# Reciprocal denominators carried by DMAs through a DRAM scratch instead of spread by matmuls, with the output matmuls gathered in one burst

## The chip, the core and the metric

The kernel runs on one core of a Trainium2 chip. The metric is the device time of one execution in microseconds (us), and medians are quoted. The **span** is what one profiled execution shows from its first to its last instruction; the time is a little longer than the span.

## The reference

A linear attention (16 heads of 28 columns) is multiplied by a gated feed-forward branch and added to the input. There are 2048 tokens, 448 columns and 1792 hidden columns, in bfloat16.

```python
xn = layernorm(x)
q, k, v = heads(xn @ wqkv)
pq, pk = phi(q), phi(k)            # phi(t) = (t + 1 if t > 0 else exp(t)) + 1e-6
kv  = sum over tokens of pk outer v
z   = sum over tokens of pk
den = pq . z + 1e-6                # one number for each token and head
s = (pq @ kv / den) @ wo
h = relu(xn @ w1 + b1) ** 2
g = silu(h @ w2 + b2)
out = x + s * g
```

## The kernel before

Everything is kept transposed: `pqT[:, c, tokens]` holds 128 columns of pq on the partitions, for c = 0 to 2, and `pqx` holds the last 64. `kv` and `wo` are folded into one matrix `msb`, so that the attention output of a tile of 128 tokens (an "S tile") is pq / den times `msb`. A "gate tile" is 14 accumulating matmuls with `w2`. The division happens on pq, before the S matmuls, so the reciprocal of each (head, token) must reach the 28 partitions of its head. The kernel before does this on TensorE, with a 0/1 matrix `ehd` (row = head, column = column of the model):

```python
def spread(c):                     # ... cut: c == 3 uses two half-width matmuls for each g
    for g in range(NG):            # 32 rows of the array each: another array tiling
        r = slice(32 * g, 32 * g + 32)
        last = e.matmul(ps(bufs[g])[:, 0:512], ehd[r, c * P : (c + 1) * P], rden[r, :], ...)
    ...
    for g in range(NG):            # and VectorE multiplies pqT by what stands in PSUM
        e.tensor_tensor(out=sl, in0=sl, in1=ps(bufs[g])[:, 0:n], op=ALU.mult)
```

`ehd` is built at the start by one memset and four selects on GpSimd. Each S tile ends in a gate product (VectorE, from PSUM), an addition of x and an output DMA on the SyncE queue, which issues in order:

```python
def gate(si, b, lo, hi, k, final):
    add("dve", ... ob = ps(b)[:, lo:hi] * gs ...)
    add("dve" if final else "pool", ... ob = ob + x_tok[:, si, lo:hi] ...)   # pool is GpSimd
    dma("sp", tok(out, si, si + 1)[:, 0, lo:hi], ob, ...)
```

The second half of TensorE's program, in order:

```python
den(); quads("H3.8 H3.9 H3.10 H3.11")
# gate tiles 0..3 follow
spread(0); fold_wv(); ggs(4); spread(1); [fold_wo(c) for c in range(4)]; ggs(5)
spread(2); ggs(6); ggs(7); spread(3)
ss4_rests_last(0); ss4(1)                 # S groups of four tiles
for si in range(8, 15): ggs(si)           # gate tiles
ss4(2)
us = s_tails([(12, 0, D), (13, 0, D), (14, 0, D), (15, 0, D)])
for k in range(3):
    s_main(us[k], k, k > 0)               # third argument False: tile 12 is added on GpSimd
gg_part(15, 0, 224); s_main(us[3], 3, True, 0, 224)
gg_part(15, 224, D); s_main(us[3], 4, True, 224, D)
```

The list is laid out for the engines by a scheduler inside the kernel's program, so "in order" means the order on TensorE. One detail matters later: in both kernels every DMA has a semaphore of its own.

Of the kernel before, what the change touches and what calls it, by code (L numbers as in the profile page):

```python
# [6 lines left out]
ALU = mybir.AluOpType  # L7
AF = mybir.ActivationFunctionType

P = 128  # L10
S, D, F = 2048, 448, 1792
NT, NG, NF = S // 128, S // 512, F // 128
NH, DH = 16, 28
HC = 4
PD = 112
NGB, NOB = 8, 8

LAT = 0.12
PSUM_BANKS = 8
# [280 lines left out]
def bass_recurrent_scan__linear_attn_block__dense_activation_squared_relu__prompt_kernel(  # L300
    nc, A_x, A_wqkv, A_wo, B_x, B_w1, B_b1, B_w2, B_b2, out
):
    with ExitStack() as es:
# [8 lines left out]
        zmask = sb("zmask", [P, 5, 32], f32)  # L312
        ones = sb("ones", [P, 1], bf)
        wz = sb("wz", [P, P], bf)
        ehd = sb("ehd", [P, D], bf)
        x_tok = sb("x_tok", [P, NT, D], bf)
        wqh = sb("wqh", [P, 64], bf)
        xn = sb("xn", [P, NT, 512], bf)
# [19 lines left out]
        eps5 = sb("eps5", [P, 1], f32)  # L338
        r2 = sb("r2", [P, NF, S], bf)
        kvm = sb("kvm", [P, 4, D], bf)  # L340
        msb = sb("msb", [P, 4, D], bf)
        zsb = sb("zsb", [P, 5, 32], bf)
        lnd = sb("lnd", [P, 512], f32)[:, :]
        rden = sb("rden", [P, 512], bf)
# [9 lines left out]
        def free_ap(ap, dims):  # L354
            return bass.AP(tensor=ap.tensor, offset=ap.offset, ap=[ap.ap[0]] + dims)
# [4 lines left out]
        def select(view, name, pattern, base, cm, fill, op=ALU.is_ge, dur=0.3, after=()):  # L360
            pool(
                lambda e, _: e.affine_select(
                    out=view, in_=view, pattern=pattern, compare_op=op, fill=fill, base=base, channel_multiplier=cm
                ),
                [name], [name, *after], dur=dur,
            )
# [5 lines left out]
        def vset(ap, val, name, again=False, dur=0.08):  # L372
            add("dve", lambda e, _: e.memset(ap, val), [name] if again else [], [name], dur)
# [2 lines left out]
        pr.ops[-1].prio = -1e6  # L376
        vset(hmask[:, :], 1.0, "hmask", dur=0.15)
        vset(zmask[:, :, :], 1.0, "zmask", dur=0.2)
        vset(ehd[:, :], 0.0, "ehd", dur=0.3)
        vset(kvm[:, :, :], 0.0, "kvm", dur=1.0)  # L380
        pool(lambda e, _: e.memset(ones[:, :], 1.0), ["ones"], dur=0.1)
        pool(lambda e, _: e.memset(eps6[:, :], 1e-6), ["eps6"], dur=0.1)
# [12 lines left out]
        def head_masks(after):  # L395
            hv = hmask[:, :].rearrange("p (b j) -> p b j", b=HC)
            select(hv, "hmask", [[-DH, HC], [0, DH]], 0, 1, 0.0, after=after)
            select(hv, "hmask", [[DH, HC], [0, DH]], DH - 1, -1, 0.0, after=after)
            ev = ehd[:, :].rearrange("p (h j) -> p h j", h=NH)
            for g in range(NG):  # L400
                select(ev, "ehd", [[-1, NH], [0, DH]], -32 * g, 1, 1.0, ALU.not_equal, dur=0.6, after=after)

        tok = lambda t, lo, hi: t[0].rearrange("(p s) d -> p s d", s=NT)[:, lo:hi, :]

        def dma(eng, dst, src, writes, nbytes, reads=(), dur=0.45):
            op = add(eng, lambda e, _: e.dma_start(dst, src), reads, writes, dur, nbytes=nbytes)
            if eng == "act":
                op.prio = -1000.0 + len(pr.ops)
# [442 lines left out]
        def fold_wo(c):  # L851
            b = Buf("M")
            hs = {0: (0, 1), 1: (1, 2), 2: (2, 3), 3: (3,)}[c]

            def f(e, _):
                last = None
                for o in range(1 if c < 3 else 2):
                    dst = ps(b)[:, 0:D] if c < 3 else ps(b)[64 * o : 64 * o + 64, 0:D]
                    wd = P if c < 3 else 64
                    for h in hs:  # L860
                        last = e.matmul(  # L861
                            dst, kvm[0:PD, h, c * P : c * P + wd], w_o[0:PD, h, :], start=(h == hs[0]),
                            stop=(h == hs[-1]),
                        )
                return last

            add("pe", f, ["kvd", "kvm", "wo"], [b], 0.19 * len(hs) * (2 if c == 3 else 1))

            def ev(e, eng):
                if eng == "dve":  # L870
                    return e.tensor_copy(msb[:, c, :], ps(b)[:, 0:D])
                return e.activation(out=msb[:, c, :], in_=ps(b)[:, 0:D], func=AF.Copy)

            add("dve", ev, [b], [("msb", c)], 0.62, alts=[("act", 0.55)])

        denb = Buf("DEN")

        def den():
            def f(e, _):
# [26 lines left out]
                [denb, "eps6", "actw"], ["lnd"], 0.7,  # L906
            )
            add(
                "act", lambda e, _: e.activation(out=rden[:, :], in_=lnd, func=AF.Exp, scale=-1.0), ["lnd"],
                ["rden"], 0.65,  # L910
            )

        def spread(c):
            bufs = [Buf("RB") for _ in range(NG)]

            def f(e, _):
                last = None
                for g in range(NG):
                    r = slice(32 * g, 32 * g + 32)
                    if c < 3:  # L920
                        last = e.matmul(  # L921
                            ps(bufs[g])[:, 0:512], ehd[r, c * P : (c + 1) * P], rden[r, :], start=True, stop=True
                        )
                    else:
                        for o in (0, 1):
                            d4 = rden[r, o * P : o * P + P]
                            last = e.matmul(
                                ps(bufs[g])[64 * o : 64 * o + 64, 0:256], ehd[r, 384:448],
                                free_ap(d4, [[2 * P, 2], [1, P]]), start=True, stop=True,
                            )  # L930
                return last

            add("pe", f, ["rden", "ehd"], bufs, 0.22).mode = "row32"
            for g in range(NG):
                if c < 3:
                    sl, n, nm = pqT[:, c, g * 512 : (g + 1) * 512], 512, ("pq", g, c)
                    rd, wr = [nm], [nm]
                else:
                    sl = pqx[:, g // 2, 2 * (g % 2) : 2 * (g % 2) + 2, :].rearrange("p a b -> p (a b)")
                    n = 256  # L940
                    rd, wr = [("pqx", g // 2)], [("pqy", g)]
                add(
                    "dve",
                    lambda e, _, sl=sl, b=bufs[g], n=n: e.tensor_tensor(  # L944
                        out=sl, in0=sl, in1=ps(b)[:, 0:n], op=ALU.mult
                    ),
                    [bufs[g]] + rd, wr, 0.68 if c < 3 else 0.41,
                )

        def gg(si):  # L950
# [80 lines left out]
        def ss4(i, final=()):  # L1031
            t = 4 * i
            pe_four(*(sunit(si, si in final) for si in (t, t + 2, t + 1, t + 3)))
# [182 lines left out]
        for i in range(12, 16):  # L1216
            zsum(i)
        quads("Q2.0 H3.4 Q2.1 H3.6 Q2.2 H3.5 Q3.0 H3.7 Q3.1 H3.12 Q3.2 H3.13")
        qx(0)
        qx(1)  # L1220
        token_sum(3)
# [2 lines left out]
        z_cols()  # L1224
        token_sum(2)
        den()
        quads("H3.8 H3.9 H3.10 H3.11")
        silu_set()
        for si in range(4):
            silu(si)  # L1230
# [1 line left out]
        def ggs(si):  # L1232
            gg(si)
            silu(si)

        spread(0)
        fold_wv()
        ggs(4)
        spread(1)
        for c in range(4):  # L1240
            fold_wo(c)
        ggs(5)
        spread(2)
        ggs(6)
        ggs(7)
        spread(3)
        ss4_rests_last(0)
        ss4(1)
        for si in range(8, 15):
            ggs(si)  # L1250
        ss4(2)
        us = s_tails([(12, 0, D), (13, 0, D), (14, 0, D), (15, 0, D)])
        for k in range(3):
            s_main(us[k], k, k > 0)
        gg_part(15, 0, 224)
        s_main(us[3], 3, True, 0, 224)
        gg_part(15, 224, D)
# [31 lines left out]
```

## Time and profile before

| | before |
|---|---|
| time, median of 6 runs | 146.93 us (146.86 to 147.61) |
| span of the profiled execution | 145.1 us |
| last denominators' start to last S matmul's start | 50.76 us, TensorE never waiting |
| last S matmul's start to last output issue | 1.99 us |
| last output issue to the span's end | 2.1 us |

Where TensorE makes nearly the whole chain that ended last, a change elsewhere is worth only what TensorE no longer does and what happens behind its last matmul. So the reader is to measure slots, from one start to the next: durations overlap, as the ends of matmuls are modelled. The prediction below shows the lines.

### The profile page before, as it was taken

How to read it: one execution, taken by the hardware profiler on the slowest of the kernel's cores; microseconds unless marked ns; L12 is line 12 of the kernel's file. 1: busy time of each engine (PE TensorE's matmuls, PEld its weight loads, DVE VectorE, ACT ScalarE, POOL GpSimd, SP SyncE). 2: the span in 40 equal slices, each digit the busy share in tenths (PEclk: the TensorE clock that was granted, in tenths of full speed). 3: DMA queues.
4: the chain of work that ended last, by engine and by line, in shares of the span. 5: the costliest groups of instructions: out<-in, count | busy, mean ns of one | idle time of the engine just before them, and what ended most of it. 6: DMA issues, size and time to landing. Idle time of an engine off the chain costs nothing.

```text
span 145.1 us, 2851 instructions
## 1 busy us (share of the span) xinstructions
PE 140.2 (97%) x1134; PEld 72.5 (50%) x1134; DVE 95.7 (66%) x218; ACT 78.2 (54%) x150; POOL 36.5 (25%) x55
## 2 busy tenths in 40 slices
PE   7999999999999999999999999999999999999990
PEld 7774444444455444444444454464444455554490
DVE  5869989899985177678999500089847913123792
ACT  3618897988884198869879412598411012212010
POOL 2123025470000487003540000000000991000590
PEclk9999999999999999999999999999999999999999
DMA  3977899920744100000000000000000232000034
GB/s 94 315 240 234 209 183 374 340 84 0 52 97 103 41 5 0 0 0 5 2 0 0 5 0 0 0 5 2 0 0 0 65 104 88 0 0 0 5 127 127
DMA packets 16025, 10.53 MB, mean 73 GB/s; under 512 B 7500, under 2 KB 15628, under 8 KB 16012
## 3 DMA queue, kind: packets, MB, share of 16 engines
q1 hardware_dynamic: 15824, 10.28, 26.6%
q8 instruction: 9, 0.15, 0.4%
q10 hardware_dynamic: 188, 0.07, 0.2%
q14 instruction: 4, 0.03, 0.1%
HBM read 6.94 MB, written 1.84 MB: 60 GB/s over the span
## 4 chain that ended last, share of the span: by engine, by line
PE 96%; DVE 1%; ACT 1%; issue 0%
PE pb L957 28%; PE pb L716 26%; PE pb L624 7%; PE pb L785 6%; PE pb L650 6%; PE pb L1026 6%; PE pb L712 3%; PE pb L1114 3%; PE pb L979 2%; PE pb L1099 1%; PE pb L664 1%; PE pb L861 1%; PE pb L791 1%; PE pb L921 1%; PE pb L813 1%; PE pb L883 1%
## 5 line engine op out<-in xcount | busy, mean ns | idle before, releaser
L957 PE MATMUL pb<-w,r 128*128 128x448 bf16 x210 | 40.6, 353 | 0.0
L716 PE MATMUL pb<-xT,w 64*128 64x512 bf16 (+1 forms) x291 | 38.3, 376 | 0.0
L683 ACT ACTIVATE r<-pb,b1f 128x512 bf16<-128x512 f32 x54 | 33.7, 691 | 6.7 <-PE pb L716 6.7
L957 PEld LDWEIGHTS pb<-w,r 128*128 128x128 bf16 x210 | 20.2, 98 | 19.5 <-issue 1.2
L1015 POOL TENSOR_TENSOR obuf<-obuf,x_tok 128x448 bf16<-128x448 bf16 x13 | 13.1, 1043 | 53.9 <-DVE obuf L1009 53.9
L999 ACT ACTIVATE gbuf<-gbuf 128x448 bf16<-128x448 bf16 x15 | 8.3, 579 | 26.2 <-DVE gbuf L966 26.1
L716 PEld LDWEIGHTS pb<-xT,w 64*128 64x128 bf16 (+1 forms) x291 | 14.2, 94 | 16.5 <-ACT r L683 0.4
L966 DVE TENSOR_TENSOR gbuf<-pb,b2b 128x448 bf16<-128x448 f32 x15 | 9.4, 625 | 19.3 <-PE pb L957 19.2
L634 POOL TENSOR_TENSOR zacc<-zacc,pk 128x448 f32<-128x448 f32 x13 | 14.5, 1116 | 18.9 <-DVE pk L614 18.4
L697 DVE TENSOR_TENSOR r<-r 128x512 bf16<-128x512 bf16 x37 | 17.4, 502 | 2.0 <-ACT r L683 1.9
L624 PE MATMUL pb<-w_qkv,xT 64*128 64x448 bf16 x112 | 13.2, 349 | 0.0
L944 DVE TENSOR_TENSOR pqT<-pqT,pb 128x512 bf16<-128x512 bf16 x12 | 7.4, 681 | 7.2 <-PE pb L921 7.2
L602 ACT ACTIVATE pk<-pb 128x448 bf16<-128x448 f32 x16 | 7.8, 541 | 7.7 <-PE pb L624 7.7
L698 ACT ACTIVATE r<-r 128x512 bf16<-128x512 bf16 x19 | 11.2, 633 | 0.0
L650 PE MATMUL pb<-xT,w_qkv 64*128 64x512 bf16 x84 | 11.0, 376 | 0.0
L1009 DVE TENSOR_TENSOR obuf<-pb,gbuf 128x448 bf16<-128x448 f32 (+1 forms) x17 | 9.0, 590 | 2.6 <-PE pb L1026 2.4
L716 PE MATMUL pb<-xT,w_1r 64*128 64x512 bf16 x56 | 10.3, 377 | 0.0
L614 DVE SCALAR_TENSOR_TENSOR pk<-pb,pk 128x448 bf16<-128x448 f32 x16 | 9.9, 624 | 0.5
L466 DVE BATCH_NORM_STATS2 st<-x_tok 128x6 f32<-128x448 bf16 x16 | 9.2, 614 | 1.4 <-DMA x_tok<-in_A_x_dram 1.4
L785 PE MATMUL pb<-pk,xn 128*128 128x448 bf16 x48 | 9.4, 353 | 0.0
L607 DVE TENSOR_SCALAR pk<-pk 128x448 bf16<-128x448 bf16 x16 | 6.0, 377 | 4.3 <-ACT pk L602 4.2
L624 PEld LDWEIGHTS pb<-w_qkv,xT 64*128 64x128 bf16 x112 | 5.4, 94 | 6.1 <-issue 0.4
(92 smaller groups left out, 134.5 us busy)
## 6 DMA issues: line engine op xcount, KB each, us to landing
out_dram<-obuf SPq DMA_DIRECT2D x15, 112.0 KB, 1.7
w<-in_B_w_dram SPq DMA_DIRECT2D x1, 1568.0 KB, 9.5
x_tok<-in_A_x_dram SPq DMA_DIRECT2D x3, 448.0 KB, 4.4
w<-in_B_w_dram SPq DMA_DIRECT2D x3, 384.0 KB, 4.2
w_qkv<-in_A_wqkv_dram SPq DMA_DIRECT2D x3, 336.0 KB, 5.6
w_o<-in_A_wo_dram SPq DMA_DIRECT2D x1, 392.0 KB, 8.9
w_qkv<-in_A_wqkv_dram SPq DMA_DIRECT2D x6, 56.0 KB, 5.1
x_tok<-in_A_x_dram SPq DMA_DIRECT2D x2, 112.0 KB, 2.1
```

The lines of the kernel that those rows point to most:

```text
L614: lambda e, _: e.scalar_tensor_tensor(out=slot, in0=ps(buf)[:, 0:n], scalar=1.0 + 1e-6, in1=slot, op0=ALU.add, op1=ALU.max),
L624: return e.matmul(ps(b)[:, 0:D], xT[rw, si, c, :], w_qkv[rw, c, D : 2 * D], start=start, stop=stop)
L634: lambda e, _: e.tensor_tensor(out=o[:, 0:D], in0=pk[:, 0, :] if i == 1 else zacc[:, :], in1=pk[:, i, :], op=ALU.add),
L650: return e.matmul(ps(b)[:, 0:512], w_qkv[rw, c, m * P : (m + 1) * P], xT[rw, 4 * g : 4 * g + 4, c, :], start=start, stop=stop,)
L683: rl = lambda e, _: e.activation(out=slot, in_=ps(b)[:, 0:512], func=AF.Relu, bias=b1f[:, fi : fi + 1])
L697: return e.tensor_tensor(out=slot, in0=slot, in1=slot, op=ALU.mult)
L698: return e.activation(out=slot, in_=slot, func=AF.Square)
L716: return e.matmul(ps(b)[:, 0:512], lhs, xT[rw, 4 * g : 4 * g + 4, c, :], start=start, stop=stop, skip_group_check=not full,)
L785: last = e.matmul(ps(b)[:, 0:D], xn[:, si, c * P : (c + 1) * P], pk[:, si, :], start=(si == 0), stop=(si == NT - 1),)
L957: last = e.matmul(ps(b)[:, 0:D], r2[:, fi, si * P : (si + 1) * P], w_2[:, fi, :], start=(fi == 0), stop=(fi == NF - 1),)
L966: lambda e, _: e.tensor_tensor(out=gbuf[:, si % NGB, :], in0=ps(b)[:, 0:D], in1=b2b[:, :], op=ALU.add),
L1015: lambda e, _: e.tensor_tensor(out=ob, in0=ob, in1=x_tok[:, si, lo:hi], op=ALU.add),
```

## The change

The intent is to take from TensorE the four spreads and the changes of array tiling around them. The reciprocals are stored to DRAM (4 stores), and 22 loads, each of one head's row repeated on up to 28 partitions, lay them out in the SBUF room of `pk`, which is dead by then. VectorE then multiplies two SBUF operands. So that the loads have time, all three S groups stand in one burst behind gate tile 12; this needs more gate and output buffers, for which `msb` moves into `at`. Tile 12's last addition moves from GpSimd to VectorE. Two smaller edits are among the lines cut below: the scheduler's assumed cost of a DMA issue rises from 0.45 to 0.6 us, and ScalarE's Exp writes the reciprocals in another order of columns. The diff, cut to its core:

```diff
-NGB, NOB = 8, 8
+NGB, NOB = 13, 10
-        ehd = sb("ehd", [P, D], bf)
+        rsp = nc.dram_tensor("rden_rows", [NH, 2, 1024], bf)
-        msb = sb("msb", [P, 4, D], bf)
+        msb = at
-        vset(ehd[:, :], 0.0, "ehd", dur=0.3)
-            for g in range(NG):
-                select(ev, "ehd", [[-1, NH], [0, DH]], -32 * g, 1, 1.0, ALU.not_equal, dur=0.6, after=after)
-        def spread(c):
 ... (cut)
+        def store_rden():
+            for g in range(NG):
+                dma("sp", rsp.ap()[:, :, g * 256 : (g + 1) * 256], rden[32 * g : 32 * g + NH, :]..., ["rden"])
+        def load_rden(c):
 ... (cut: for each head h in the 128 rows of c)
+                    dma(("sp", "act")[len(queue) % 2], rb[p : p + n, 2048 * c : 2048 * c + cols],
+                        bass.AP(tensor=rsp, offset=h * 2048 + src0, ap=[[0, n], [1, cols]]), ...)
+        def divide(c):
+            for v in (0, 1):
 ... (cut: sl is 1024 columns of pqT, or 512 of pqx; r the same of rb)
+                e.tensor_tensor(out=sl, in0=sl, in1=r, op=ALU.mult)
+        quads("H3.8 H3.9 H3.10 H3.11")
         qx(0)
 ... (cut)
         den()
-        quads("H3.8 H3.9 H3.10 H3.11")
+        store_rden()
+        for c in range(4):
+            load_rden(c)
 ... (cut: gate tiles 0 to 3; then, spreads left out, gate tiles 4, 5, 6 and the folds)
+        for si in range(7, 13):
+            ggs(si)
+        for c in range(4):
+            divide(c)
+        ss4(0)
         ss4(1)
-        for si in range(8, 15):
-            ggs(si)
         ss4(2)
         us = s_tails([(12, 0, D), (13, 0, D), (14, 0, D), (15, 0, D)])
-        for k in range(3):
-            s_main(us[k], k, k > 0)
+        ggs(13)
+        s_main(us[0], 0)
+        ggs(14)
+        s_main(us[1], 1)
+        s_main(us[2], 2)
```

More of the change, by code (lines that the diff above doesn't have):

```diff
@@ L398, in head_masks, with dma @@
             select(hv, "hmask", [[DH, HC], [0, DH]], DH - 1, -1, 0.0, after=after)
-            ev = ehd[:, :].rearrange("p (h j) -> p h j", h=NH)
-            for g in range(NG):
-                select(ev, "ehd", [[-1, NH], [0, DH]], -32 * g, 1, 1.0, ALU.not_equal, dur=0.6, after=after)
         tok = lambda t, lo, hi: t[0].rearrange("(p s) d -> p s d", s=NT)[:, lo:hi, :]
-        def dma(eng, dst, src, writes, nbytes, reads=(), dur=0.45):
+        def dma(eng, dst, src, writes, nbytes, reads=(), dur=0.6):
             op = add(eng, lambda e, _: e.dma_start(dst, src), reads, writes, dur, nbytes=nbytes)
@@ L872, in ev @@
                 return e.activation(out=msb[:, c, :], in_=ps(b)[:, 0:D], func=AF.Copy)
-            add("dve", ev, [b], [("msb", c)], 0.62, alts=[("act", 0.55)])
+            add("dve", ev, [b], [("msb", c), ("at", c)], 0.62, alts=[("act", 0.55)])
         denb = Buf("DEN")
@@ L908, in den @@
             add(
-                "act", lambda e, _: e.activation(out=rden[:, :], in_=lnd, func=AF.Exp, scale=-1.0), ["lnd"],
-                ["rden"], 0.65,
-            )
-        def spread(c):
-            bufs = [Buf("RB") for _ in range(NG)]
-            def f(e, _):
-                last = None
-                for g in range(NG):
-                    r = slice(32 * g, 32 * g + 32)
-                    if c < 3:
-                        last = e.matmul(
-                            ps(bufs[g])[:, 0:512], ehd[r, c * P : (c + 1) * P], rden[r, :], start=True, stop=True
-                        )
-                    else:
-                        for o in (0, 1):
-                            d4 = rden[r, o * P : o * P + P]
-                            last = e.matmul(
-                                ps(bufs[g])[64 * o : 64 * o + 64, 0:256], ehd[r, 384:448],
-                                free_ap(d4, [[2 * P, 2], [1, P]]), start=True, stop=True,
-                            )
-                return last
-            add("pe", f, ["rden", "ehd"], bufs, 0.22).mode = "row32"
-            for g in range(NG):
+                "act",
@@ new lines, in den @@
+                lambda e, _: e.activation(
+                    out=rden[:, :].rearrange("p (o j t) -> p j o t", o=2, j=2),
+                    in_=lnd.rearrange("p (j o t) -> p j o t", o=2, j=2), func=AF.Exp, scale=-1.0,
+                ),
+                ["lnd"], ["rden"], 0.65,
+            )
+        rb = pk[:, :, :].rearrange("p a b -> p (a b)")
+        def store_rden():
+            for g in range(NG):
+                dma(
+                    "sp", rsp.ap()[:, :, g * 256 : (g + 1) * 256],
+                    rden[32 * g : 32 * g + NH, :].rearrange("p (o x) -> p o x", o=2), [("rd", g)], NH * 1024, ["rden"],
+                )
@@ new lines, in load_rden @@
+        def load_rden(c):
+            done = [o for o in pr.ops if o.eng in ("pe", "pool") and ("pk", NT - 1) in o.reads]
+            parts = [(0, P * c, P, 0, 2048)] if c < 3 else [(64 * v, P * c, 64, 1024 * v, 1024) for v in (0, 1)]
+            for p0, f0, rows, src0, cols in parts:
+                f = f0
+                while f < f0 + rows:
+                    h = f // DH
+                    n = min((h + 1) * DH, f0 + rows) - f
+                    name = ("rb", c, p0, h)
+                    p = p0 + f - f0
+                    queue.append(0)
+                    dma(
+                        ("sp", "act")[len(queue) % 2], rb[p : p + n, 2048 * c : 2048 * c + cols],
+                        bass.AP(tensor=rsp, offset=h * 2048 + src0, ap=[[0, n], [1, cols]]), [name], n * cols * 2,
+                        [("rd", g) for g in range(NG)],
+                    )
+                    op = pr.ops[-1]
+                    op.prio = None
+                    op.deps.update(done)
+                    for d in done:
+                        d.succ.append(op)
+                    names.setdefault(c, []).append(name)
+                    f += n
@@ L935, in spread @@
+        queue = []
+        names = {}
+        def divide(c):
+            for v in (0, 1):
                 if c < 3:
-                    sl, n, nm = pqT[:, c, g * 512 : (g + 1) * 512], 512, ("pq", g, c)
-                    rd, wr = [nm], [nm]
-                else:
-                    sl = pqx[:, g // 2, 2 * (g % 2) : 2 * (g % 2) + 2, :].rearrange("p a b -> p (a b)")
-                    n = 256
-                    rd, wr = [("pqx", g // 2)], [("pqy", g)]
-                add(
-                    "dve",
-                    lambda e, _, sl=sl, b=bufs[g], n=n: e.tensor_tensor(
-                        out=sl, in0=sl, in1=ps(b)[:, 0:n], op=ALU.mult
-                    ),
-                    [bufs[g]] + rd, wr, 0.68 if c < 3 else 0.41,
+                    sl = pqT[:, c, v * 1024 : (v + 1) * 1024].rearrange("p (j o t) -> p j o t", o=2, t=P)
+                    o = 2048 * c + v * 512
+                    r = free_ap(rb[:, o : o + P], [[P, 4], [1024, 2], [1, P]])
+                    rd = wr = [("pq", g, c) for g in (2 * v, 2 * v + 1)]
+                else:
+                    sl = pqx[:, v, :, :].rearrange("p a b -> p (a b)")
+                    r = rb[:, 6144 + 512 * v : 6656 + 512 * v]
+                    rd, wr = [("pqx", v)], [("pqy", 2 * v), ("pqy", 2 * v + 1)]
+                add(
+                    "dve", lambda e, _, sl=sl, r=r: e.tensor_tensor(out=sl, in0=sl, in1=r, op=ALU.mult), rd + names[c], wr,
+                    0.78 if c < 3 else 0.42,
@@ L1234, in ggs @@
             silu(si)
-        spread(0)
+        ggs(4)
         fold_wv()
-        ggs(4)
-        spread(1)
+        ggs(5)
         for c in range(4):
             fold_wo(c)
-        ggs(5)
-        spread(2)
         ggs(6)
-        ggs(7)
-        spread(3)
-        ss4_rests_last(0)
+        for si in range(7, 13):
[3 more added lines that the diff above has]
+        ss4(0)
         ss4(1)
-        for si in range(8, 15):
-            ggs(si)
         ss4(2)
         us = s_tails([(12, 0, D), (13, 0, D), (14, 0, D), (15, 0, D)])
-        for k in range(3):
-            s_main(us[k], k, k > 0)
+        ggs(13)
[3 more added lines that the diff above has]
+        s_main(us[2], 2)
         gg_part(15, 0, 224)
```

## The prediction

> **What bounds the kernel now.** I read the page's busy shares first, then the chain that ended last, then TensorE's timeline from the denominators on, and at the end the tail on VectorE, GpSimd and the SyncE queue.
>
> ```profile
> span 145.1 us, 2851 instructions
> PE 140.2 (97%) x1134; PEld 72.5 (50%) x1134; DVE 95.7 (66%) x218; ACT 78.2 (54%) x150; POOL 36.5 (25%) x55
> PE 96%; DVE 1%; ACT 1%; issue 0%
> ```
>
> TensorE is busy 97% of the span and makes 96% of the chain, so elsewhere time is worth nothing unless it makes TensorE wait or lies behind its last matmul. As a busy row could hide slow matmuls, I checked the rate. Columns of the next view: start, duration (the modelled end overlaps the next start), engine, line, operation.
>
> ```profile
> 98.29 0.40 PE L921 MATMUL pb<-rden,ehd 32*128 32x512 bf16 x4
> 98.61 1.62 PE L861 MATMUL pb<-w_o,kvm 112*128 112x448 bf16 x8
> 100.17 2.82 PE L957 MATMUL pb<-w,r 128*128 128x448 bf16 x14
> 102.92 0.39 PE L921 MATMUL pb<-rden,ehd 32*128 32x512 bf16 x4
> 103.25 5.47 PE L957 MATMUL pb<-w,r 128*128 128x448 bf16 x28
> 108.65 0.32 PE L927 MATMUL pb<-rden,ehd 32*64 32x256 bf16 x8
> 108.89 2.44 PE L1026 MATMUL pb<-msb,pqT 64*128 64x448 bf16 x24
> ...
> 114.35 18.71 PE L957 MATMUL pb<-w,r 128*128 128x448 bf16 x98
> 132.99 0.74 PE L1026 MATMUL pb<-msb,pqT 64*128 64x448 bf16 x6
> ...
> 135.65 0.54 PE L1082 MATMUL pb<-msb,pqx 64*128 64x448 bf16 x4
> ```
>
> The reader is to subtract starts. Seven gate tiles (L957) take 132.99 - 114.35 = 18.64 us; one alone between two spreads takes 102.92 - 100.17 = 2.75. Six more cost 15.89, so a gate tile streams in 2.65 us (0.189 us per matmul) and each run of them pays about 0.10 once, at the change to another array tiling. TensorE never waits in this half: its time is slots plus changes of tiling.
>
> The tail is the second thing to see. VectorE's last add and the SyncE queue's last output issue:
>
> ```profile
> 142.02 0.28 DVE L1015 TENSOR_TENSOR obuf<-obuf,x_tok 128x224 bf16<-128x224 bf16 x1
> ```
>
> ```profile
> 142.99 0.45 SPq L406 DMA_DIRECT2D out_dram<-obuf  x1
> ```
>
> The data are ready at 142.30, but the issue comes at 142.99, 0.69 late. The queue issues in order, and the output of tile 12, added on GpSimd, heads it:
>
> ```profile
> 139.95 1.18 POOL L1015 TENSOR_TENSOR obuf<-obuf,x_tok 128x448 bf16<-128x448 bf16 x1
> ```
>
> That add ends at 141.13; then five outputs go out, the first at 141.16, the last at 142.99, so 0.46 us each: (142.99 - 141.16) / 4.
>
> **What the Trainium skill says.** (1) "TensorEngine Tiling (Array Packing)", Key Properties: a change of tiling mode, not of tile, drains TensorE. The trace agrees, with the 0.10 us above. (2) "DMA: Bandwidth & Descriptors", Issuing engines are not separate DMA queues: transfers issued from several engines run on the same 16 DMA engines, and a second issuer saves only issue time. This trace cannot show it (its two queues hardly overlap); I take from it that the two queues help the 22 issues, not the bytes. (3) "SBUF — State Buffer", Who interferes with whom: VectorE and GpSimd contend for one port pair that is an exclusive lock. The trace agrees: the final add takes 0.27 us for 224 columns alone, but 1.07 mean for 448 while GpSimd adds beside it.
>
> **The change part by part.**
>
> *Spreads removed.* Slots from start to next start: 94.35 to 94.67, 98.29 to 98.61, 102.92 to 103.25, 108.65 to 108.89: 0.32 + 0.32 + 0.33 + 0.24 = 1.21 us, all on the path. The change of tiling into each spread goes too. Three follow gate tiles: 0.10 each, 0.30. One follows the H3.8 to H3.11 matmuls: these 28 took 94.35 - 91.22 = 3.13, against 8 such in 0.863 elsewhere, 3.02 for 28; 0.11 more. Together 0.41.
>
> *S groups in one burst.* Group 2 alone costs 135.65 - 132.99 = 2.66 us. Groups 0 and 1 cost 114.35 - 108.89 = 5.46, which is 0.14 over twice that: the exit to gate tiles, plus the order that puts the rests last. In one burst this exit goes (the last group is followed by tails of the same tiling, as now), and the entry that stays is counted in a gate run. Saved 0.14.
>
> *H3.8 to H3.11 moved ahead of the QX matmuls.* The same matmuls; nothing saved beyond the above. They no longer bridge the wait for the reciprocals, but the next work, gate tile 4, does not need these. The fold of wv needs the last token sum evacuated (0.54 us on ScalarE) and has the 2.65 us gate tile ahead of it. No new TensorE gap.
>
> Sum on TensorE: 1.21 + 0.41 + 0.14 = 1.76 us.
>
> *Tail.* Tile 12's final add moves to VectorE, so GpSimd has 12 adds of about 0.99 us (8 in 7.95 in the first burst). The burst's first gate product comes 2.3 us after its start (135.29 - 132.99), takes 0.6, so GpSimd ends near 2.9 + 12 x 0.99 = 14.8 us after the burst began. TensorE then still has 4 us: the burst takes 8.0, tails 0.47, gate tile 13 2.65, its S 0.57, tile 14 2.65, two S 1.14, and the last part, as now from 137.84 to the last slot's end near 141.29, 3.45: 18.9. So no late GpSimd add heads the output queue, and the last issue should follow its add at once: 0.65 saved. The last chain itself (last S, product 0.39, add 0.28, transfer) is unchanged.
>
> *Added transfers.* Four stores and 22 loads. Loads move 384 rows of 4 KB and 128 rows of 2 KB, 1.83 MB. The trace's best slice reaches 374 GB/s, so 4.9 us at least; issues of this kind took 0.35 to 0.60 us, so 11 on each queue take 4 to 6.6 us. Denominators end near 94.3 as now (work only swaps places before them); Ln and Exp took 0.69 and 0.63, so the reciprocals stand at 95.8, stores land near 99.5, loads near 106 to 109. The burst starts after gate tiles 4 to 12 (9 x 2.65), the fold of wv (0.87) and of wo (1.55): 94.3 + 26.3 = 120.6. Slack is some 12 us.
>
> *VectorE.* Twelve multiplies of 0.68 from PSUM and four of 0.41 become six of 1024 columns and two of 512. Squares of 512 columns from SBUF took 0.42 and the 224-column add 0.27, a slope of 0.52 ns a column, so an estimated 0.69: 6 x 0.69 + 2 x 0.42 = 5.0 instead of 9.8 us. Off the path: nothing.
>
> *ScalarE.* Eleven issues at about 0.57 (0.53 to 0.61 for the two like ones at the start), 6.3 us, and a wait for the stores in order. It has 24 us to the burst for 1.3 of table, 2.2 of evacuation and some 7 us of silu: hidden. The removed memset and selects stood before idle time: nothing.
>
> Sum: span 145.1 - 1.76 - 0.65 = 142.7. Time over span is 146.95 - 145.1 = 1.85, so 144.5; I add 0.1 for small new bank waits (second rival): **144.6 us**, 1.6% less.
>
> **The rivals.**
>
> *Loads late.* If broadcasts from one row ran at a quarter of the best rate, 1.83 MB would take 20 us and the burst wait about 7 us: 150 or more. For it: no transfer before reads one 4 KB row 28 times. Against: the weights, in rows of 896 bytes, already reach the 374 GB/s above, and 12 us of slack must go first. A milder form: VectorE, in order, sits on an early divide while gate products wait; with eight PSUM banks and 2.65 us per gate tile, it could sit for over 10 us before TensorE feels it.
>
> *PSUM banks in the burst.* Twelve S tiles want banks at 0.66 us each; gate products clear one each 0.53 to 0.57 us. The tails need four banks 8.0 us in; group 1 should be cleared by 7.3. Gate tile 13 wants one at 8.4, which the first product of group 2 frees at 8.2. That is a near miss; if VectorE is behind with divides or bias adds, TensorE loses 0.5 to 1.5 us here and nothing is left of the burst's worth: 145 to 146. This is the likeliest way to miss high.
>
> *The tail gain fails.* If the adds of tiles 13 and 14 bunch up before the last output, or the transfers of the burst still occupy the queue, the 0.65 is lost: 145.2.
>
> *More gain than counted.* Below 144.0 would need 0.5 us that I cannot find on TensorE; an earlier start, through the changed model of issue cost reordering the early instructions, could give some tenths, or take them.
>
> **Range and chances.** The TensorE sum is differences of starts, good to 0.2. The tail may fail whole (+0.65), the burst may stall (+0.5 to 1), early reordering may move 0.3 either way. So 144.0 to 145.8 holds 8 in 10. Two per cent faster is below 144.0: 0.13. Slower by 2% needs the loads to be late: 0.03. Within: 0.84.
>
> **What would show it.** TensorE busy near 138.5 us with 20 matmuls fewer; gate tiles 6 to 12 in one run of about 18.6; 42 S pairs' slots (84 matmuls) in about 8.0 us with no wait; gate tile 13 right after the tails. Last load landed before 110, divides before 115. VectorE near 5 us less. The last output issue within 0.1 us of the last add. A TensorE gap before the burst names the loads; one inside it or at tile 13 names the banks; a late last issue names the tail. I am wrong in kind if the time falls through work ahead of the denominators, or if TensorE's sum holds but the time does not.

## The result and the profile after

The changed kernel takes **145.08 us** (median of 6 runs, 144.92 to 145.21) against 146.93 us: ratio 0.9866, 95% interval 0.9848 to 0.9885. Ratios here are the mean time of one kernel's fast runs over the mean of the other's of the same rounds, so they are not quite the ratio of the medians. The output is correct. The prediction's 144.6 us was 0.5 us low, and its range holds the result.

The page of the kernel after: the head, the busy share of the DMA engines (in tenths) and the GB/s that they moved in each fortieth of the span, and the shares of the chain that ended last.

```profile
span 143.1 us, 2830 instructions
PE 138.0 (96%) x1114; PEld 72.4 (51%) x1114; DVE 92.5 (65%) x212; ACT 77.1 (54%) x148; POOL 32.7 (23%) x50
...
DMA  3977899970452400000000000001499200024341
GB/s 80 315 247 201 173 240 337 338 170 0 41 111 55 92 0 5 0 0 0 5 0 0 5 0 0 0 0 23 124 174 179 39 0 5 0 75 149 116 144 33
...
PE 93%; DVE 2%; DMA 1%; ACT 1%; issue 0%
```

TensorE has 20 matmuls fewer and remains the bound. The bytes of the new transfers are the five neighbouring values 23, 124, 174, 179 and 39. Each slice is 3.58 us, so in no slice do the loads pass 179 GB/s, although the DMA engines were as busy (9) as in the early slices that moved 337 and 338 GB/s.

TensorE's timeline of the kernel after, from the gate tile behind the denominators on (start, duration, engine, line, operation):

```profile
94.43 2.82 PE L972 MATMUL pb<-w,r 128*128 128x448 bf16 x14
97.09 0.99 PE L809 MATMUL pb<-at,w_qkv 128*112 128x112 bf16 x16
97.91 2.81 PE L972 MATMUL pb<-w,r 128*128 128x448 bf16 x14
100.56 1.61 PE L857 MATMUL pb<-w_o,kvm 112*128 112x448 bf16 x8
102.10 18.71 PE L972 MATMUL pb<-w,r 128*128 128x448 bf16 x98
120.75 0.74 PE L1041 MATMUL pb<-at,pqT 64*128 64x448 bf16 x6
...
128.70 0.54 PE L1097 MATMUL pb<-at,pqx 64*128 64x448 bf16 x4
129.18 2.82 PE L972 MATMUL pb<-w,r 128*128 128x448 bf16 x14
...
139.35 0.45 PE L1114 MATMUL pb<-at,pqT 128*128 128x224 bf16 x3
```

No line has an idle time in brackets: TensorE never waits here. Seven gate tiles take 120.75 - 102.10 = 18.65 us as before; the burst of 84 S matmuls takes 128.70 - 120.75 = 7.95 us.

VectorE's multiplies, first and last (the brackets give the wait before and what ended it):

```profile
111.78 0.69 DVE L961 TENSOR_TENSOR pqT<-pqT,pk 128x1024 bf16<-128x1024 bf16 x1 [3.54 <-DMA pk<-rden_rows]
...
117.33 0.42 DVE L961 TENSOR_TENSOR pqx<-pqx,pk 128x512 bf16<-128x512 bf16 x1
```

The first has waited 3.54 us for loads: the milder form of the prediction's late-loads rival did occur, and TensorE did not feel it. The last ends at 117.75, 3.0 us before the burst. The new tail, VectorE's last addition and SyncE's last issue:

```profile
140.36 0.27 DVE L1030 TENSOR_TENSOR obuf<-obuf,x_tok 128x224 bf16<-128x224 bf16 x1
140.66 0.33 SPq L402 DMA_DIRECT2D out_dram<-obuf  x1
```

The issue now follows the end of the addition (140.63) by 0.03 us. Before, it was 0.69 late.

**Where the time came from**, by differences of starts in the two traces. The denominators start later by the 3.02 us of the H3.8 to H3.11 matmuls, which were moved ahead of them and are counted out on both sides.

| stretch | before | after | difference |
|---|---|---|---|
| span's start to the denominators, without the H3 work | 90.24 | 90.43 | +0.19 |
| denominators to the last S matmul's start, without it | 47.74 | 45.90 | -1.84 |
| last S matmul's start to the last output issue | 1.99 | 1.31 | -0.68 |
| last issue to the last output's landing | 1.63 | 1.52 | -0.11 |
| last landing to the span's end | 0.47 | 0.87 | +0.40 |
| time less span, mean | 1.75 | 2.07 | +0.32 |
| sum | | | -1.72 |

The means (146.83 us in the larger set of runs of before, 145.07 us) differ by 1.76 us. The two savings make 2.52 us, and 0.8 us comes back in three other places: at the start, behind the last issue, and outside the span. The experiments are about both.

### The profile page after: what moved, and what is told of

Read it like the earlier page. It is cut to its first block, busy times and chain, and to the rows that moved or that the text cites. A ratio compares the mean times of both kernels' runs of the same rounds, so it can differ in the third digit from the quotient of the medians.

```text
span 143.1 us, 2830 instructions
## 1 busy us (share of the span) xinstructions
PE 138.0 (96%) x1114; PEld 72.4 (51%) x1114; DVE 92.5 (65%) x212; ACT 77.1 (54%) x148; POOL 32.7 (23%) x50
## 4 chain that ended last, share of the span: by engine, by line
PE 93%; DVE 2%; DMA 1%; ACT 1%; issue 0%
PE pb L972 28%; PE pb L712 27%; PE pb L620 7%; PE pb L781 6%; PE pb L646 6%; PE pb L1041 6%; PE pb L708 3%; PE pb L994 2%; DMA x_tok<-in_A_x_dram 1%; PE pb L1114 1%; PE pb L660 1%; PE pb L787 1%; PE pb L857 1%; DVE st L462 1%; PE pb L809 1%; PE pb L879 1%
## 5 line engine op out<-in xcount | busy, mean ns | idle before, releaser
L1030 POOL TENSOR_TENSOR obuf<-obuf,x_tok 128x448 bf16<-128x448 bf16 x12 | 12.1, 1044 | 49.4 <-DVE obuf L1024 49.4
L693 DVE TENSOR_TENSOR r<-r 128x512 bf16<-128x512 bf16 x37 | 18.3, 523 | 2.9 <-ACT r L679 2.9
L610 DVE SCALAR_TENSOR_TENSOR pqT<-pb,pqT 128x512 bf16<-128x512 f32 x12 | 8.2, 689 | 0.3
```

What stands on the lines that cost most here:

```text
L610: lambda e, _: e.scalar_tensor_tensor(out=slot, in0=ps(buf)[:, 0:n], scalar=1.0 + 1e-6, in1=slot, op0=ALU.add, op1=ALU.max),
L693: return e.tensor_tensor(out=slot, in0=slot, in1=slot, op=ALU.mult)
L1030: lambda e, _: e.tensor_tensor(out=ob, in0=ob, in1=x_tok[:, si, lo:hi], op=ALU.add),
```

## The experiments

My theory: the two savings stand on their own (fewer slots and tiling changes on TensorE; an output queue that is no longer held up), and the loads are hidden. Rivals: the tail gained through something else than the queue; the tiling changes cost less than assumed, and the gain was an accident of order; the DMAs are paid for somewhere.

### The changed kernel again

Edit: none.

> The changed kernel once more, nothing edited, as a second trace of it beside the parts. All theories: ratio to before 0.985 to 0.989. In the first trace the first weights (w, first 384 KB) landed at 6.73 us instead of 6.40 before and the program's epilogue after the last landing took 0.33 us longer. If these two are chance of one execution, this trace shows other values (landing anywhere from 6.3 to 6.8) with the same total within 0.2 us; if they belong to the program, they return within 0.05 us.

Measured: 144.92 us, ratio 0.9874 (0.9855 to 0.9893). The result repeats. Time less span is 2.09 us in the mean, and the program's end is again longer: in the trace's records, SyncE's last branch to its drain takes 0.47 us, against 0.16 in the kernel before (0.49 in the first trace after). The expectation's 0.33 us is this step alone; from the last landing to the span's end, it is 0.38 us more than before here. So the time outside the span and the longer end are properties of the program. The first weights landed at 6.91 us after the span's start, later than in either first trace (6.40 before, 6.73 after), and this landing varies by 0.8 us among the traces of all kernels (6.14 to 6.91).

### The tail alone

```diff
 # on the kernel before
-            s_main(us[k], k, k > 0)
+            s_main(us[k], k, True)
```

> The kernel before with one edit: tile 12's final add on VectorE instead of GpSimd. Queue theory (a late GpSimd add heads the output queue and costs the last issue 0.69 us): if tile 12's engine alone is what matters, the last issue follows the last add within 0.1 us and the time falls by 0.6 to 0.7 us, ratio 0.9955. Rival (it is the earlier burst, which lets GpSimd finish earlier, that empties the queue): VectorE's adds still stand beside GpSimd's to about 140 us and are slowed there, the outputs still bunch, and the gain is 0 to 0.3 us, ratio 0.998 to 1.000.

Measured: 145.98 us, ratio 0.9952 (0.9935 to 0.9969). VectorE's last addition in this kernel's timeline:

```profile
141.78 0.28 DVE L1015 TENSOR_TENSOR obuf<-obuf,x_tok 128x224 bf16<-128x224 bf16 x1
```

It ends at 142.06, 0.24 us earlier than in the kernel before, where the last matmul started 0.23 us later too. But the last issue comes at 142.11, directly behind it, so from the last S matmul's start to it there are 1.34 us instead of 1.99. One word in the program gives 0.65 us in this stretch, and 0.7 us in the means of the runs: the queue was held up by the addition at its head, as the prediction had read it. The rival (another addition slowed by a shared port) was half right as to the cause and wrong as to the effect: a VectorE addition still took 1.22 us beside a GpSimd one, but the queue just caught up.

### The order alone

```diff
 # on the kernel before, spreads kept; also NGB, NOB = 13, 10 and msb = at for room
-        ss4_rests_last(0); ss4(1)
-        for si in range(8, 15): ggs(si)
+        for si in range(8, 13): ggs(si)
+        ss4(0); ss4(1)
         ss4(2)
 ...     # tails, then gate tiles 13 and 14 among the last S tiles, as in the change
```

> The kernel before with the new order of the end (three S groups behind gate tile 12, tiles 13 and 14 between the tails) and its larger buffers, but with the reciprocals still spread by matmuls. My theory: 0.14 us on TensorE (the last S matmul starts 0.1 to 0.2 earlier) and 0.65 in the tail, so 0.8 us in all, ratio 0.9945. Rival (all of the gain comes from the removed matmuls and the order is worth nothing): ratio 0.999 to 1.001.

Measured: 145.89 us, ratio 0.9936 (0.9922 to 0.9951). From the denominators to the last S matmul TensorE takes 50.61 us against 50.76, so the one burst is worth 0.15 us (0.14 expected); the last issue follows the last S matmul by 1.32 us, so the tail is worth 0.67. Time less span is 1.76 us, as before. The order alone has no hidden price.

### The DMAs alone

```diff
 # on the kernel after
-        for si in range(7, 13):
+        for si in range(7, 12):
             ggs(si)
 ...     # divides
-        ss4(0)
+        ss4_rests_last(0)
         ss4(1)
+        for si in range(12, 15): ggs(si)
         ss4(2)
 ...     # tails
+        for k in range(3): s_main(us[k], k, k > 0)      # tile 12 on GpSimd again
```

> The changed kernel with the reciprocals spread by DMA, but the S groups in the old way: groups 0 (rests last) and 1 together, now behind gate tile 11 so that the loads are in, group 2 behind tile 14, tile 12's final add on GpSimd. My theory: the spread slots and their changes of tiling are gone, 1.62 us on TensorE, and the tail of before returns, last issue 0.6 to 0.7 us behind the last add: 1.4 to 1.7 us faster than before, ratio 0.9895. If the parts add up, the gains of this run and of the order-only run sum to the whole, 1.85 to 2.5 us. Rival (the matmuls were cheap and the burst made the gain): ratio above 0.995.

Measured: 146.37 us, ratio 0.9966 (0.9952 to 0.9979): only 0.5 us gained. **This is a clear miss**. The two lines that carry the tail:

```profile
140.70 0.27 DVE L1030 TENSOR_TENSOR obuf<-obuf,x_tok 128x224 bf16<-128x224 bf16 x1
...
141.69 0.44 SPq L402 DMA_DIRECT2D out_dram<-obuf  x1
```

TensorE did save what was expected: 46.17 + 3.02 = 49.19 us from the denominators to the last S matmul, 1.57 less than before. The tail lost its gain, as it should (data ready at 140.97, issue at 141.69). But the start was 0.26 us later, the stretch from the last landing to the span's end 0.39 us longer (0.32 of it between SyncE's last branch and its drain), and time less span 2.23 us, 0.48 more. So the DMA part, whose TensorE saving is real, has a price of about 1.1 us elsewhere. The next runs look for it.

### Four more pairs of tiling changes

```diff
 # on the kernel after
+        # one 1-column matmul in the 32-row tiling, behind each of gate tiles 7 to 10
         for si in range(7, 13):
             ggs(si)
+            if si < 11:
+                other_tiling()
```

> The changed kernel with one 1-column matmul in the 32-row tiling put behind each of gate tiles 7, 8, 9 and 10; its result is not used. It measures the disputed size of a change of tiling: a spread was said to be 0.21 to 0.22 us of streaming and the rest changes, each about 0.10. My theory: every one costs two changes and a slot of some 0.03, 0.23 us, so the seven gate tiles take 18.64 + 0.92 = 19.6 us and the time rises by 0.9 us over the changed kernel (ratio to before 0.993). Rival (changes of tiling are free and the 0.41 us were something else, waits for banks or for the reciprocals): under 0.15 us in all.

Measured: 145.97 us, ratio 0.9936 (0.9917 to 0.9956), which is about 0.9 us more than the kernel after. In its timeline on TensorE:

```profile
107.65 0.17 PE L1258 MATMUL pb<-wz,ident 32*128 32x1 bf16 x1
107.76 2.82 PE L972 MATMUL pb<-w,r 128*128 128x448 bf16 x14
110.51 0.17 PE L1258 MATMUL pb<-wz,ident 32*128 32x1 bf16 x1
```

The stage takes 19.49 us instead of 18.64. Each insertion costs 0.21 us for two changes of tiling and a matmul of a single column, so a change costs about 0.10 us, whatever the work in it. This is the size that the prediction used. That the tilings are free falls.

### One queue for each half of the partitions (single look)

```diff
-                        ("sp", "act")[len(queue) % 2], rb[...], ...
+                        ("sp", "act")[p >= 56], rb[...], ...
```

> The changed kernel with each load's queue chosen by where it lands: partitions 0 to 55 from SyncE, the rest from ScalarE, so that two loads in flight write different halves; same bytes, same result. In the changed kernel the loads took from 100.8 to 113.3 us, 147 GB/s in the mean, packets of 4 KB 173 ns when alone and 300 to 340 ns beside others. If the written partitions are what is crowded, the last load lands 2 to 5 us earlier. If reading one row 28 times, or the number of engines per load, is the limit, it lands within 1 us of 113.3. The time stays as it was, 145.0 +- 0.2, either way, as the loads have 3 us of slack.

Measured: 145.11 us, state unknown. The last load lands 11.8 us after the first issue instead of 12.5. So crowding of the written partitions explains at most 0.7 of the 12.5 us.

### Distinct rows instead of one row 28 times (single look, wrong result on purpose)

```diff
-                        bass.AP(tensor=rsp, offset=h * 2048 + src0, ap=[[0, n], [1, cols]]), ...
+                        bass.AP(tensor=rsp, offset=0, ap=[[1024, n], [1, cols]]), ...
```

> The changed kernel with each load reading its partitions' rows from different addresses, 2 KB apart, instead of one row over and over; a wrong result on purpose, same bytes, same count, same destinations. Choosing the queue by partition half moved the last landing by only 1.0 us. If reading one 4 KB row 28 times is what holds the loads at about 150 GB/s, they now run at 250 to 370 GB/s and the last one lands 4 to 7 us earlier, near 107 to 109; if it is the shape of the loads (28 rows at a time, few engines or few destinations at once), it lands within 1 us of 113.

Measured: 144.89 us, relative error 0.098 as intended. The last load lands 11.8 us after the first issue (112.4 against 100.6). Reading one DRAM row 28 times over is not the main limit either. What is left is the shape of the loads (28 rows or fewer at a time) and that two queues send at once, and no run isolates these. The packet records in the kept traces point to the second. In the kernel after, a 4 KB packet of the loads took 0.17 us (median) when no packet of the other queue started within 0.4 us of it, and 0.32 us when one did; in all eleven traces with these loads it is 0.16 to 0.19 against 0.25 to 0.32 us. A run with all loads on one queue is missing, so this stays a correlation.

### The transfers alone, their data unused

```diff
 # on the kernel before
         den()
+        store_rden()
+        for c in range(4):
+            load_rden(c)
 # and gate tile 14's bias addition waits for them
```

> The kernel before, matmul spreads and all, with the change's 4 stores and 22 loads added and their data unused (only the bias add of gate tile 14, at about 130 us, waits for them). It prices the transfers by themselves. In all three traces with these transfers the last stretch from the last output's landing to the end took 0.84 us instead of 0.45, and time minus span was 2.08 to 2.23 us instead of 1.75. Theory: a fixed price of the 26 transfers, so this kernel is 0.6 to 0.7 us slower than before, ratio 1.0040 to 1.0050, with 0.3 to 0.5 of it outside the span. Rival (the price belongs to the order, or is chance): ratio 0.999 to 1.001, time minus span 1.75.

Measured: 147.23 us, ratio 1.0026 (1.0012 to 1.0039): the 26 transfers alone cost 0.4 us, less than the 0.6 to 0.7 us expected. TensorE's timeline is unmoved (last S matmul at 141.00, as before), and SyncE's last issue stands where it stood:

```profile
143.00 0.44 SPq L407 DMA_DIRECT2D out_dram<-obuf  x1
```

The span ends at 145.5, so 2.5 us later instead of 2.1. In the trace's records the branch-to-drain step at the program's end takes 0.48 us. Time less span is 1.71 us: **not** raised. So the transfers bring the price at the program's end, and something else brings the price outside the span.

### The 26 transfers on five semaphores

```diff
 # on the kernel after: one shared semaphore for the stores, one for each 128-row group of loads;
 # who waits, waits for the whole group's count
-                    op.sem, op.seq, op.key = es.enter_context(nc.semaphore(f"d{n_dma}")), 16, ("d", n_dma)
+                    op.sem, op.key = shared[op.group]
+                    op.seq = 16 * sum(o.group == op.group for o in self.ops)
```

> The changed kernel with the same 26 transfers counted on 5 semaphores instead of 26 (one for the stores, one for the loads of each 128 rows; the waits are for the full count). If the fixed price of the transfers is one of semaphores, it goes: 0.5 to 0.7 us faster than the changed kernel, ratio to before 0.9825 to 0.9835, time minus span back to 1.75 to 1.8. If it is one of the transfers themselves or of the longer instruction streams: ratio 0.986 to 0.988 as the changed kernel, time minus span 2.05 to 2.1.

Measured: 144.65 us, ratio 0.9845 (0.983 to 0.9861), 0.4 us less than the kernel after, where 0.5 to 0.7 us were expected. The last output issue:

```profile
140.56 0.33 SPq L410 DMA_DIRECT2D out_dram<-obuf  x1
```

It comes 0.10 us earlier than in the kernel after, but the span ends at 142.6, only 2.0 us later (after: 2.4). The branch-to-drain step is back at 0.15 us with the same bytes moved. So the price at the end, 0.39 us from the last landing (0.34 of it in this step), goes with the 21 further semaphores and the waits on them, not with the transfers. The edit also takes 14 instructions out of the program (2830 to 2816), so whether the number of semaphores or that of the instructions counts is not told apart. Time less span stays at 2.06 us: that it would fall too was wrong.

### S groups 0 and 1 four gate tiles earlier (single look)

```diff
 # on the kernel after
-        for si in range(7, 13):
+        for si in range(7, 9):
             ggs(si)
 ...     # divides
         ss4(0); ss4(1)
+        for si in range(9, 13): ggs(si)
         ss4(2)
```

> The changed kernel with S groups 0 and 1 behind gate tile 8 instead of 12 (group 2 stays behind 12), 10.6 us earlier, so that the slack of the loads turns negative. The prediction put the last load at 106 to 109 us; with that TensorE, ready at 110.1, would wait 1 to 3 us for the divides and the time be 146 to 148. The changed kernel's trace puts the last load at 113.3 and the last divide at 117.7: then TensorE waits 6 to 7 us and the time is 151 to 152.5.

Measured: 152.84 us, in an execution of unknown state with a mean granted clock of 0.977. On TensorE, with the page's row of the granted clock (tenths, for each fortieth of the span):

```profile
PEclk9999999999999999999999999999995599999999
...
114.89 1.30 PE L1041 MATMUL pb<-at,pqT 64*128 64x448 bf16 x6 [4.45 <-DVE pqx L961]
```

TensorE waits 4.45 us for VectorE's divides, which wait for the loads. The two groups then take 123.03 - 114.89 = 8.1 us instead of 5.3, with a lowered clock. The wait lies between the two that were expected (1 to 3 us by the prediction's landing, 6 to 7 us by the first trace), and the total is above both. The late-loads rival of the prediction exists: it is one change of order away. The further cost behind the wait (about 2.8 us) is the lowered clock: by the trace's `--windows` view the granted clock was 0.50 from 113.7 to 120.5 us, so the 5.6 us of S matmuls in that time, at half speed, lost 2.8 us. The drop began 3.3 us into the wait; one execution can't show that the wait caused it.

### A combined version, and its base

The base starts from the five-semaphore kernel and makes two more cuts. The last fold of `wo` (c = 3) becomes one matmul of 128 columns from a doubled copy of its 64 columns, instead of two of 64 in another tiling. And the last tile is cut at column 320 instead of 224, so that the chain behind the last matmul handles 128 columns. The combined version also puts the removed memset and four selects of `ehd` back. They compute a matrix that nothing reads.

```diff
 # base, and combined too
-                for o in range(1 if c < 3 else 2): ...      # two 64-column matmuls for c == 3
+                    lhs = kvm[0:PD, h, c * P : c * P + P] if c < 3 else kx[0:PD, :]
-        gg_part(15, 0, 224); s_main(us[3], 3, True, 0, 224); gg_part(15, 224, D); s_main(us[3], 4, True, 224, D)
+        gg_part(15, 0, 320); s_main(us[3], 3, True, 0, 320); gg_part(15, 320, D); s_main(us[3], 4, True, 320, D)
 # combined only
+        ehd = sb("ehd", [P, D], bf)
+        vset(ehd[:, :], 0.0, "ehd", dur=0.3)
+            for g in range(NG): select(ev, "ehd", ...)
```

> As the combined kernel, but without the memset and the four selects put back. (a) and (b) as there: 0.45 us faster than five semaphores alone, ratio to before 0.9815, time minus span 2.05. If time minus span is the same in both, the missing GpSimd work is not what raised it, and what raised it stays open.

> Five semaphores for the 26 transfers, plus three edits. (a) The fold of wo for the last 64 columns as one 128-column matmul from a doubled copy of its weights instead of two in the 64-column tiling: its stage falls from 1.54 to 1.33 us, as two changes of tiling go. (b) The last tile cut at 320 columns instead of 224: the last chain behind TensorE (silu, product, add) falls from 0.36 + 0.39 + 0.27 to some 0.31 + 0.25 + 0.20, 0.25 us less. (c) The memset and the four GpSimd selects that the change removed are put back, unused: if their absence is what raised time minus span from 1.75 to 2.06, it returns to 1.75; if not, it stays at 2.05. Together with (c) working: 0.75 us faster than with five semaphores alone, ratio to before 0.9795; without: 0.9815.

Measured: base 144.26 us, ratio 0.9829 (0.9806 to 0.9851); combined **143.79 us**, ratio 0.9794 (0.9773 to 0.9815). The combined version beats both kernels; its interval straddles the 2% line. Time less span is 2.08 us in the base and **1.77 us** in the combined version. Five instructions whose result is unused (and the tile that they write) lower the time outside the span by 0.31 us. They may help inside it too (mean spans 142.2 and 142.0), but the spans of the single runs overlap.

TensorE of the combined version, at the fold of `wo`:

```profile
100.14 1.30 PE L879 MATMUL pb<-w_o,kvm 112*128 112x448 bf16 x6
101.28 0.35 PE L879 MATMUL pb<-w_o,kx 112*128 112x448 bf16 x1
101.47 18.70 PE L993 MATMUL pb<-w,r 128*128 128x448 bf16 x98
```

The fold takes 101.47 - 100.14 = 1.33 us against 102.10 - 100.56 = 1.54 in the kernel after: one matmul and two changes of tiling less. The chain behind its last matmul:

```profile
139.02 0.28 ACT L1025 ACTIVATE gbuf<-pb 128x128 bf16<-128x128 f32 x1 [0.81 <-PE pb L1015]
139.33 0.29 DVE L1045 TENSOR_TENSOR obuf<-pb,gbuf 128x128 bf16<-128x128 f32 x1 [0.24 <-ACT gbuf L1025]
139.66 0.23 DVE L1051 TENSOR_TENSOR obuf<-obuf,x_tok 128x128 bf16<-128x128 bf16 x1
```

Product and addition take 0.29 and 0.23 us, against 0.39 and 0.27 for 224 columns.

One thing goes with the price outside the span: the page's row of a small queue for instructions (packets, MB, share). First the combined version, then the base:

```profile
q14 instruction: 4, 0.03, 0.1%
```

```profile
q14 instruction: 3, 0.02, 0.1%
```

The kernels with 4 packets in the span (before, tail alone, order alone, transfers alone, combined) have 1.71 to 1.77 us outside it; the timed kernels with 3 have 2.06 to 2.23. The packet records in the traces show where the missing packet went: in each of the nine kernels without `ehd`, two 8 KB packets of this queue start behind the span's end, the second 1.3 to 1.8 us behind it; in the five with `ehd`, none or one does. So transfers of instructions move from inside the span to behind it. That the end of an execution waits for them is not shown, no run varied it by itself, and which of the five instructions matters stays open.

## Why the prediction was right, and where it was off

**TensorE: 1.76 us predicted, 1.84 measured.** Right, and its parts hold apart: the DMAs alone gave 1.57 (1.62 by the prediction's terms for spreads and their tilings), the burst alone 0.15 (0.14), and a tiling change about 0.10 where four pairs were added. The two parts sum to 1.72; 0.12 us of the whole is not assigned.

**Tail: 0.65 predicted, 0.68 measured.** Right, and for the reason given: moving only tile 12's addition gave it, and putting it back with the old order took it away. The engine of that addition is enough; the new order was not needed for it. GpSimd's last addition ended 15.1 us after the burst's start (14.8 predicted), TensorE 18.9 after it, as predicted.

**Burst.** 7.95 us with no wait and gate tile 13 directly behind the tails: the rival of the PSUM banks did not happen, and the 0.1 us added for it was not needed.

**VectorE.** Its multiplies took 6 x 0.68 + 2 x 0.41 = 4.9 us, as estimated (5.0), off the path. The whole engine fell by 3.2 us (95.7 to 92.5), not by the "near 5" of the prediction.

**Loads: hidden, as said, but the slack was mis-sized.** The step that failed is the landing near 106 to 109 with some 12 us of slack. The stores landed at 100.8 (99.5 predicted), the loads were issued from there to 106.3, and the last landed at 113.3. Their 1.83 MB in 12.5 us are 147 GB/s, where the estimate took the best slice's 374. The prediction counted on two queues to "help the 22 issues, not the bytes"; the packets' times under "Distinct rows" suggest that they slowed the bytes. With the divides behind the loads, 3.0 us were left. This cost nothing, but a burst four gate tiles earlier stood still for 4.45 us.

**"Time over span" as a constant: a second step that failed.** The prediction took 1.85 us from one kernel's median and carried it over. In the mean it is 1.75 us before and 2.07 after. The runs show what it goes with: neither the order alone nor the transfers alone raised it, and it fell by 0.31 us where the unused memset and selects were put back (base against combined). So "the removed memset and selects stood before idle time: nothing" was wrong by 0.3 us, though they were idle work by every view of the span.

**A term that was missing: the program's end.** The last issue to the span's end was taken as unchanged; from the last landing on it grew by 0.40 us with one semaphore for each of 26 transfers, and 0.39 of that went away with five. I priced the transfers as bytes and issues, not as semaphores.

**Start.** The denominators came 0.19 us later than before. Over all traces, with the moved work counted out, they start between 90.01 and 90.36 us in the five kernels that build `ehd`, and between 90.17 and 90.64 in the nine that don't. The ranges overlap. The landing of the first weights scatters as much, but it does not explain the start (the DMA-only kernel had the earliest landing, 6.14 us, and one of the later starts, 90.50), so whether this is chance or a second effect of the removal stays open.

The sum, by the prediction's own path: 142.7 us of span, -0.08 (TensorE), -0.03 (tail), +0.19 (start), -0.11 (last landing), +0.40 (end) gives 143.1; with 2.07 in place of 1.85 + 0.1 this is 145.1, as measured.

## What to carry to other kernels

When TensorE bounds a kernel, moving a small layout job from matmuls to DMAs saves, as here, their slots and the changes of tiling (about 0.1 us each), and this can be read off in advance as differences of starts. But compare the span's last stretch and the time outside the span too: when a change adds many DMAs, let those with a common reader share a semaphore (with a wait for the full count), and look for gains in the order of the output queue, where here a single addition on the wrong engine cost 0.65 us. A part that was removed because nothing waited for it can still change the total, so remove such parts in a run of their own.

## What the Trainium skill lacked or had wrong

- "TensorEngine Tiling (Array Packing)", Key Properties: it says that a change of mode drains TensorE, and the runs agree, but it gives no duration. Here a change costs about 0.10 us: four pairs, with one 1-column matmul each, added 0.85 us to a stage.
- "DMA: Bandwidth & Descriptors", How many engines (k): by its rule a load of 28 rows runs on 14 of the 16 engines, and the traces agree (behind a first step 0.5 to 0.8 us after the start of the issue, the semaphore of such a load rises 14 times; 12 times for 24 rows and 10 for 20). This would explain a loss of an eighth, but the loads reached 147 GB/s, against 374 GB/s in the best slice of the kernel before. Neither distinct source rows nor separate halves of the partitions changed much (11.8 us for the loads each, against 12.5). What the page does not give is how long a packet takes while a second queue sends: here 0.32 us for 4 KB, against 0.17 us alone.
- "Runtime: NRT & Kernel Launch", The launch sequence: it gives each stage around a kernel one duration, and none is said to depend on how many semaphores the kernel uses. Here 21 further semaphores, with the waits on them, lengthened the end of the program by 0.34 us inside the span (0.49 against 0.15 us from SyncE's last branch to its drain).
- No page has it: time outside the span differs among versions of one kernel. It was 1.77 us with one memset and four selects that were off every path, and 2.08 us without them.
